# Value matmuls of 512 queries instead of 2 x 256, with new rules of the build-time scheduler, in a four-layer attention stack

## The chip, the cores and the metric

The kernel runs on one core of one Trainium2 chip. The metric is the device time of one execution in microseconds (us), the median of several runs. Besides these runs there is one profiled execution with a trace of every instruction of the engines: PE (matmuls; PEld are its weight loads), DVE (VectorE), ACT (ScalarE), POOL (GpSimd) and SP (which issues nearly all DMAs here).

## The reference

A sequence of 2048 tokens of width 512 goes through four layers A, B, A, B, each added to its input after a layer norm. Layer A is ordinary attention with 32 heads of width 16; layer B is a linear attention with a learned feature map ("Hedgehog").

```python
q, k, v = ...(x @ wqkv)                       # 32 heads, Dh = 16, S = 2048
# A:
scores = einsum("bhqd,bhkd->bhqk", q, k) * Dh ** -0.5
o = einsum("bhqk,bhkd->bhqd", softmax(scores), v);   out = o @ wo
# B:
phi_q = concat(softmax(q @ w_phi), softmax(-q @ w_phi));  phi_k likewise
kv = einsum("bhsf,bhsd->bhfd", phi_k, v);  z = sum_s phi_k
o = (phi_q @ kv) / (phi_q @ z + 1e-6);               out = o @ wo
x = x + A(ln(x)); x = x + B(ln(x)); x = x + A(ln(x)); x = x + B(ln(x))
```

## The kernel before, in words

What the change touches is `LayerA.attention`, which runs once for each of the two A layers. The work of one A layer is cut into 32 groups G; a group is a set of four heads (`g`, 8 of them) and a block of 512 queries (`j`, 4 of them). Inside a group a loop goes over 16 blocks of 128 keys (`kt`), and each key block has two halves of two heads. One half is one **tile**:

- `scores` (L1151): eight small f16 matmuls write the scores of 2 heads x 128 keys x 512 queries to one of two PSUM tiles `s`. I call these eight matmuls a score S. Two tiles `s` exist, so a score can only start when the exponential two tiles earlier has read its tile.
- one exponential on ACT (L1158) turns `s` into `p` (128 x 1024, f32) in SBUF. There are six buffers `p`.
- `pvs` (L1202) multiplies `p` by the values and adds to the group's accumulator: one call takes both halves of one key block, but only 256 of the 512 queries (`part` 0 or 1), in eight f32 matmuls. I call the work of both parts, a whole key block, a V; before, it is written as two halves. A buffer `p` is free when the V that reads it is done.

A layer has 32 x 16 x 2 = 1024 tiles. About one tile in 45 gets its exponential on DVE and POOL instead (`power_task`, buffer `px`); the rest are ACT's.

The accumulator of a group lies in one of two double banks of PSUM, called `double` and `pm` in the profile. The same two banks carry all **side products**: chains of up to twelve units of eight matmuls (`mm_cols`, L685) that compute q, k and v of the next heads or, late in a layer, the output projection; and the transposes of the next layer's input. `take` gives out a bank, `freed` gives it back when DVE has copied the result out of it. After a group's last V, DVE does that with two transposes (L850) in `norm_task`.

The order of all PE, DVE, ACT and POOL instructions is written out at build time (`tc.manual_schedule`): the loop in `attention` keeps a model clock for PE and ACT (`UNIT` is a score or a side unit, `PVHALF` half a V, `EXP` an exponential, `THERE` the time from a score's start to its exponential, `BACK` from an exponential's start to its tile `s` being free) and a second model, `Plan`, for DVE and POOL. At each step it emits a score if a tile is free, else a V, a side unit or a power score, if that fits before the next score is due. What the engines then do follows from the order and the semaphores alone; each engine runs its instructions strictly in order.

The output projection of a layer's first three quarters of the heads reads the normed outputs back from DRAM: `load_ob(j)` issues the DMA of `ob` (and, for j = 0, of the weights `woA`), and `part(j)` emits the side units that use it, 8 us of the model clock later.

In the first layer two more streams run beside the attention: `prep_b` (folds a feature map into weights of layer B, on PE and DVE, through the tiles `xt`) and `prep_rest` (splits the output weights of A, `prep_ao`, then the weights of B).

```python
            f = slice(256 * part, 256 * part + 256)
            ...
                    nc.tensor.matmul(acc[h][32 * hh:32 * hh + 32, f], self.oct[o]["v"][r, x:x + 32],
                                     pt[r, hh % 2, f], start=(kt == 0 and part == 0), stop=(kt == NT - 1), skip_group_check=True)
```

## Time and profile before

| | us |
|---|---|
| median of 3 runs | 2597.81 (2591.81 to 2602.13) |
| the profiled execution: time / span | 2605.12 / 2603.3 |
| mean granted PE clock, of full speed | 0.974 |
| busy in the span: PE / ACT / DVE / POOL | 2377.6 / 2135.1 / 1559.6 / 635.7 |
| ACT in the exponentials of L1158, 2003 of them: busy / idle before | 1852.3 / 111.3 |
| first layer A, first to last exponential | about 71 to 1057 |
| second layer A, first to last exponential | about 1377 to 2352 |

The two layers A take some 1960 of the 2603 us. A busy share is an average over stages: PE is shown busy in 91% of the span, but the matmuls' ends are modelled, and inside the layers A it is the chain of exponentials on ACT that has to be followed. An idle time in a row stands with what ended it ("<-PE s L1151": ACT waited for a score; "<-issue": the engine waited for nothing that the profile shows).

### The profile page before, as it was taken

How to read it: one execution, taken by the hardware profiler on the slowest of the kernel's cores; microseconds unless marked ns; L12 is line 12 of the kernel's file. 1: busy time of each engine (PE TensorE's matmuls, PEld its weight loads, DVE VectorE, ACT ScalarE, POOL GpSimd, SP SyncE). 2: the span in 40 equal slices, each digit the busy share in tenths (PEclk: the TensorE clock that was granted, in tenths of full speed). 3: DMA queues.
4: the chain of work that ended last, by engine and by line, in shares of the span. 5: the costliest groups of instructions: out<-in, count | busy, mean ns of one | idle time of the engine just before them, and what ended most of it. 6: DMA issues, size and time to landing. Idle time of an engine off the chain costs nothing.

```text
span 2603.3 us, 136308 instructions
## 1 busy us (share of the span) xinstructions
PE 2377.6 (91%) x63082; PEld 1380.2 (53%) x63082; DVE 1559.6 (60%) x2745; ACT 2135.1 (82%) x2381; POOL 635.7 (24%) x735
## 2 busy tenths in 40 slices
PE   6799999999988899899788999999899889998998
PEld 4466566555644555445345655565565556554543
DVE  8456556635664346889964564564455432557897
ACT  5799899999998899444437999999999889994453
POOL 3122222221120000356431222212121110004553
PEclk9899999999999999999888999999999999999999
DMA  5300421131044422100133003203300351210003
GB/s 195 59 18 8 92 54 38 29 50 35 5 103 112 157 96 68 50 17 17 66 100 53 18 8 61 33 5 48 66 5 12 75 143 53 69 52 25 9 17 107
DMA packets 114637, 144.96 MB, mean 56 GB/s; under 512 B 64152, under 2 KB 69896, under 8 KB 111624
## 3 DMA queue, kind: packets, MB, share of 16 engines
q1 hardware_dynamic: 112872, 133.38, 20.9%
q8 instruction: 495, 8.11, 1.3%
q0 software_dynamic: 1184, 2.77, 0.3%
q14 instruction: 86, 0.70, 0.1%
HBM read 62.16 MB, written 41.94 MB: 40 GB/s over the span
## 4 chain that ended last, share of the span: by engine, by line
ACT 46%; PE 24%; DVE 12%; issue 12%; SPq 3%; POOL 2%; DMA 1%; ACTq 0%; POOLq 0%; DVEq 0%
ACT p L1158 44%; PE s L1151 5%; PE pm L1202 4%; PE double L1202 3%; PE double L685 2%; PE pbv L1496 1%; DVE su L1566 1%; PE pk L1496 1%; PE po L668 1%; PE pm L685 1%; PE pq L1496 1%; SPq L863 1%; POOL f L1575 1%; DVE f L1558 1%; DVE st L474 1%
## 5 line engine op out<-in xcount | busy, mean ns | idle before, releaser
L1158 ACT ACTIVATE p<-s 128x1024 f32<-128x1024 f32 x2003 | 1852.3, 1106 | 111.3 <-PE s L1151 108.4
L1151 PE MATMUL s<-kq 49*32 49x512 f16 x15192 | 860.0, 386 | 63.3 <-ACT p L1158 17.4
L1202 PE MATMUL pm<-p,v 64*32 64x256 f32 x16592 | 693.1, 378 | 20.2 <-issue 19.9
L1151 PEld LDWEIGHTS <-kq 49*32 49x32 f16 x15872 | 392.7, 90 | 545.5 <-issue 407.5
L1202 PE MATMUL double<-p,v 64*32 64x256 f32 x15456 | 638.8, 380 | 3.7 <-issue 3.7
L1202 PEld LDWEIGHTS pm<-p,v 64*32 64x32 f32 x16592 | 349.0, 106 | 92.0 <-issue 34.7
L1202 PEld LDWEIGHTS double<-p,v 64*32 64x32 f32 x15456 | 320.8, 107 | 67.7 <-issue 14.1
L853 POOL TENSOR_TENSOR yt<-yt,yt 128x512 f32<-128x512 f32 x64 | 82.1, 1283 | 861.7 <-DVE yt L850 775.1
L1496 PEld LDWEIGHTS <-xnTa 128*128 128x128 f16 x1152 | 111.4, 99 | 157.3 <-DVE f L1559 29.8
L1235 DVE SCALAR_TENSOR_TENSOR xt<-double,c_oA,xt 128x512 f32<-128x512 f32 x78 | 58.1, 746 | 163.7 <-PE double L685 162.6
L1575 POOL TENSOR_TENSOR f<-f,su 128x1024 f32<-128x1024 f32 x62 | 119.8, 1933 | 132.4 <-DVE su L1569 106.1
L850 DVE STREAM_TRANSPOSE yt<-pm 128x512 f32<-128x512 f32 x66 | 43.7, 696 | 159.2 <-PE pm L1202 159.0
L850 DVE STREAM_TRANSPOSE yt<-double 128x512 f32<-128x512 f32 x62 | 41.2, 696 | 159.8 <-PE double L1202 159.8
L968 POOL TENSOR_TENSOR sq<-stg 128x512 bf16<-128x512 f16 x48 | 58.2, 1213 | 315.9 <-DVE stg L878 183.3
L1181 POOL TENSOR_TENSOR pz<-pw 128x512 f32<-128x512 f32 x90 | 103.5, 1151 | 128.3 <-DVE pw L1172 87.5
L685 PE MATMUL double<-woA,ob 64*32 64x512 f16 x2088 | 123.4, 378 | 1.7 <-issue 1.6
L1560 ACT ACTIVATE f<-f,c_pB 128x1024 f32<-128x1024 f32 x64 | 72.7, 1148 | 55.7 <-DVE f L1559 55.7
L1496 PE MATMUL pbv<-wbv,xnTa 128*128 128x512 f16 x384 | 95.4, 402 | 25.1 <-DVE f L1559 25.1
L685 PEld LDWEIGHTS <-wA 64*32 64x32 f16 x4608 | 86.4, 92 | 39.9 <-issue 2.7
L1183 DVE SCALAR_TENSOR_TENSOR px<-pz,px 128x512 f32<-128x512 f32 x90 | 82.2, 913 | 36.0 <-POOL pz L1181 28.6
L1581 ACT ACTIVATE fk<-f 128x1024 f16<-128x1024 f32 x30 | 31.7, 1057 | 72.2 <-POOL f L1575 72.2
L1496 PE MATMUL pq<-wbqk,xnTa 128*128 128x512 f16 x384 | 88.4, 379 | 0.0
(320 smaller groups left out, 3229.0 us busy)
## 6 DMA issues: line engine op xcount, KB each, us to landing
kq<-stg SPq DMA_DIRECT2D x168, 128.0 KB
xd<-xt SPq DMA_DIRECT2D x40, 512.0 KB
xt<-xd SPq DMA_DIRECT2D x40, 512.0 KB
v<-vyt SPq DMA_DIRECT2D x384, 16.0 KB
oD<-osp SPq DMA_DIRECT2D x24, 256.0 KB
ob<-oD SPq DMA_DIRECT2D x8, 768.0 KB
xt<-in_A_x_dram SPq DMA_DIRECT2D x8, 512.0 KB
wbqk<-dBqk SPq DMA_DIRECT2D x2, 2048.0 KB
```

The costliest lines, as they stand in the source:

```text
L685: nc.tensor.matmul(ps[h][c, :], w[r, c], x[r], start=(n == 0), stop=(n == of - 1), skip_group_check=True)
L850: nc.vector.transpose(ys[u].rearrange("p a b -> p (a b)"), ps[u])
L853: nc.gpsimd.tensor_tensor(ys[0], ys[0], ys[1], ALU.add)
L968: nc.gpsimd.tensor_tensor(sq, hi, hi, ALU.mult)
L1151: nc.tensor.matmul(banks2[u][32 * c:32 * c + 32, :], self.side(g, half, 64 * u, 0, kt * P + 32 * c, 32), self.side(g, half, 64 * u, 1, j * ...
L1158: nc.scalar.activation(pt, s, AF.Exp, scale=EXPS)
L1181: nc.gpsimd.tensor_tensor(z, w, w, ALU.mult)
L1183: nc.vector.scalar_tensor_tensor(y, z, PB, y, op0=ALU.add, op1=ALU.mult)
L1202: nc.tensor.matmul(acc[h][32 * hh:32 * hh + 32, f], self.oct[o]["v"][r, x:x + 32], pt[r, hh % 2, f], start=(kt == 0 and part == 0), stop=( ...
L1496: nc.tensor.matmul(dst, xnT[:, a, c, t * P:(t + 1) * P], w(b, c), start=(i == 0 and c == 0), stop=(i == 2 and c == NC4 - 1))
L1560: nc.scalar.activation(f, f, AF.Exp, scale=con["pB"])
L1575: nc.gpsimd.tensor_tensor(f3, f3, self.part_sums(f3, slice(0, 64), factor), ALU.mult)
```

## The change

One V is written as eight matmuls of 512 queries instead of sixteen of 256. With it, five things of the scheduler and its streams change:

- the model's numbers (`STEP` 0.865 for a whole V in place of twice `PVHALF` 0.434, `THERE`, `BACK`, `LATE`, and the new `SIDE` and `ALIGN`);
- a new side chain may take a bank right up to the end of a group (before, not at the group's last key block); no power tile in group 0;
- a side unit must end before the next `s` is free, not before the next score is due;
- `ob` for j = 0 is fetched from step 300 on, when the first output is stored (before: step 348), and its users come at least 22 us of the model clock after the fetch (14 for the others; before 8);
- `prep_ao` loads and splits the output weights in two halves, through the three `xt` tiles instead of two large ones, and runs after `prep_b` instead of before; the weights of B are loaded from step 356 on.

```diff
-PVHALF = 0.434
+STEP = 0.865
 EXP = 0.904
-THERE = 0.541
-BACK = 1.135
+THERE = 0.53
+BACK = 1.1
-AHEADS = 0
-LATE = 0.08
+LATE = 0.15
+SIDE = 0.0
+ALIGN = 0.05
...
     def prep_ao():
-        wo = load_w(a_wo, "awo")
+        ws = []
+        for i in range(2):
+            ws.append(xp.tile([P, 2, 512], F32, tag="xt", name=f"awo{i}"))
+            nc.sync.dma_start(ws[i], a_wo.rearrange("(c p) n -> p c n", p=P)[:, 2 * i:2 * i + 2])
...
+                    hl = xp.tile([P, 2, 2, 512], F16, tag="xt", name=f"ahlo{i}")
...
+            nc.sync.dma_start(dAo[:, :, 2 * i:2 * i + 2], hl)
...
     def prep_rest():
-        yield "until", lambda: a1.ready == 3
+        yield "until", lambda: bool(folded)
         yield from prep_ao()
-        yield "until", lambda: bool(folded)
+        yield "until", lambda: a1.now >= 356
...
-        def pvs(self, G, kt, part, acc):
+        def pvs(self, G, kt, acc):
...
-                    nc.tensor.matmul(acc[h][32 * hh:32 * hh + 32, f], self.oct[o]["v"][r, x:x + 32],
-                                     pt[r, hh % 2, f], start=(kt == 0 and part == 0), ...)
+                    nc.tensor.matmul(acc[h][32 * hh:32 * hh + 32, :], self.oct[o]["v"][r, x:x + 32],
+                                     pt[r, hh % 2, :], start=(kt == 0), ...)
...
         def part(self, j):
-                yield "gap", 8.0
+            yield "until", lambda: self.plan.now >= self.fetched[j] + (22.0 if j == 0 else 14.0)
...
-            events.append((348, lambda: "oA" in con, lambda: 0 in self.obs or self.load_ob(0)))
+            events.append((300, lambda: "oA" in con and self.ready == 3 and self.stored >= 0, lambda: 0 in self.obs or self.load_ob(0)))
...
-                    first = need is not None and need[1][0] == "pe" and (ready <= AHEADS or len(need[1]) > 2 and ready <= 3)
+                    first = need is not None and need[1][0] == "pe" and len(need[1]) > 2 and ready <= 1
...
-                                    soon = pvq and pvq[0][1] == NT - 1 or pvq and pvq[0][0] not in acc
+                                    soon = pvq and (NT - pvq[0][1] <= ALIGN * what[0] or pvq[0][0] not in acc)
...
-                                elif pe + what[0] <= max(due, free):
+                                elif pe + what[0] <= (free + SIDE if len(what) == 1 else max(due, free)):
...
-                            if (G in acc or min(self.pfree) <= pe) and pe + PVHALF <= max(due, free) + (LATE if ready > 1 else 0.0):
+                            if (G in acc or min(self.pfree) <= pe) and pe + STEP <= max(due, free) + LATE:
...
-                            if tried < G and G < POWERS and ...
+                            if tried < G and 0 < G < POWERS and ...
```

The new order, at three places. Rows that only repeat are left out ("...": the same weight load and matmul go on). First PE in the middle of a group of the first layer (`s` a score's tile, `kq` its operands, `double` here the group's accumulator, `wA`, `xnT` and `pm` a side product). Before:

```order
L1151 MATMUL s<-kq_1_990 32x512
L1202 MATMUL double<-p,v_162 32x256 x8
L685 LDWEIGHTS wA
L685 MATMUL pm_4788<-xnT_2_156,wA 32x512
...
L1151 LDWEIGHTS kq_0_989
L1151 MATMUL s<-kq_0_989 32x512
...
L1202 MATMUL double<-p,v_162 32x256 x8
```

After:

```order
L1165 MATMUL s<-kq_0_989 32x512
L1215 MATMUL double<-p,v_162 32x512 x8
L1165 LDWEIGHTS kq_1_990
L1165 MATMUL s<-kq_1_990 32x512
...
L699 LDWEIGHTS wA
L699 MATMUL pm_4901<-xnT_3_157,wA 32x512
...
L1165 LDWEIGHTS kq_0_989
```

Behind each score stood half a V and one side unit; now a whole V stands behind every second score and two side units behind the others.

Then PE at the border of groups 16 and 17 of the first layer, from the last V of the one to the first V of the other. Before (`pm` is the accumulator of both groups, `double` carries the side chain):

```order
L1202 MATMUL pm_14584<-px,v_6775 32x256
L685 LDWEIGHTS wA
L685 MATMUL double<-xnT_0_154,wA 32x512
...
L1151 MATMUL s<-kq_1_13594 32x512
...
L685 MATMUL double<-xnT_0_154,wA 32x512
...
L1151 MATMUL s<-kq_0_13593 32x512
...
L1151 MATMUL s<-kq_1_13594 32x512
L1202 MATMUL pm_15471<-p,v_6775 32x256
```

After (`double` is the accumulator of both, `pm` carries the side chain):

```order
L1215 MATMUL double<-px,v_5751 32x512 x4
L1165 LDWEIGHTS kq_0_11666
L1165 MATMUL s<-kq_0_11666 32x512
...
L699 MATMUL pm_13033<-xnT_0_154,wA 32x512
L1165 LDWEIGHTS kq_1_11667
L1165 MATMUL s<-kq_1_11667 32x512
L699 LDWEIGHTS wA
L699 MATMUL pm_13032<-xnT_0_154,wA 32x512
...
L1215 MATMUL double<-p,v_5751 32x512 x8
```

Before, three scores stand between the two V, the last two of them right ahead of the new group's first V. Now two scores do, and two side units stand between the second one and that V.

Last SP's queue where the output weights and the first outputs are fetched (`kq`: the next heads' operands, `bf`: weights of B, `oD`: outputs in DRAM). Before:

```order
L154 DMA awo<-in_A_wo_dram 128x4x512
...
L1138 DMA kq_1_20027<-sh 1x4x512 x4
L362 DMA dAo<-ahlo 128x4096
L435 DMA bf_20120<-dF_104 128x2048
L435 DMA bf_20121<-dF_105 128x2048
L689 DMA woA<-dAo 128x4096
L1209 DMA ob_20126<-oD 128x3072
```

After:

```order
L385 DMA dAo<-ahlo_9969 256x1x1024
...
L703 DMA woA<-dAo 128x4096
L800 DMA wAv<-dAv 128x1024
L957 DMA oD<-osp 128x1024
L1223 DMA ob_16271<-oD 128x3072
L449 DMA bf_16726<-dF_104 128x2048
L449 DMA bf_16727<-dF_105 128x2048
```

The weights are now stored two sets of operands (24 DMAs of `kq`) before `woA` is fetched, and `woA` and the first `ob` are ahead of the two loads `bf` that stood ahead of them.

More of the change, by code (lines that the diff above doesn't have):

```diff
@@ L323, in peaks @@
         for w in ws:
-            for d in range(NC4):
+            for d in range(w.shape[1]):
                 yield "V", 0.63, 3
@@ L835, in cols @@
         def cols(self, n, of, w, x):
-            yield "M",
+            yield "M", of
             idx, ps = self.take()
@@ L1201, in pvs @@
                     r = slice(64 * h, 64 * h + 64)
-                    nc.tensor.matmul(acc[h][32 * hh:32 * hh + 32, f], self.oct[o]["v"][r, x:x + 32],
-                                     pt[r, hh % 2, f], start=(kt == 0 and part == 0), stop=(kt == NT - 1), skip_group_check=True)
+                    nc.tensor.matmul(acc[h][32 * hh:32 * hh + 32, :], self.oct[o]["v"][r, x:x + 32],
+                                     pt[r, hh % 2, :], start=(kt == 0), stop=(kt == NT - 1), skip_group_check=True)
         def load_ob(self, j):
@@ L1208, in load_ob @@
             self.obs[j] = big([P, 3, 2, 512], F16, f"ob{j}")
+            self.fetched[j] = self.plan.now
             nc.sync.dma_start(self.obs[j], oD[j])
@@ L1437, in attention @@
                             G, kt, h = tiles[0]
-                            if tried < G and G < POWERS and pvdone >= G and kt <= 9 and min(self.pfree) <= pe and G in acc and pe + UNIT <= max(due, free):
+                            if tried < G and 0 < G < POWERS and pvdone >= G and kt <= 9 and min(self.pfree) <= pe and G in acc and pe + UNIT <= max(due, free):
                                 tried = G
```

48 lines of the change are left out of this document (27 added, 21 removed).

## The prediction, made before the change was run

> **What bounds the kernel.** I read the stage table first (busy us of each engine in four stretches of the span, in the order PE, PEld, DVE, ACT, POOL, then clock, DMA share, GB/s), then the costliest groups.
>
> ```profile
> 60.00:1100.00 1040.00, 962.62 (x29923) 577.19 (x29922) 581.82 (x1041) 941.95 (x1023) 188.16 (x195) 0.98 0.26 62
> 1370.00:2400.00 1030.00, 959.34 (x29879) 566.03 (x29878) 530.87 (x931) 945.81 (x1027) 189.10 (x185) 0.98 0.21 45
> L1158 ACT ACTIVATE p<-s 128x1024 f32<-128x1024 f32 x2003 | 1852.3, 1106 | 111.3 <-PE s L1151 108.4
> 2199.63 100.56 ACT L1158 ACTIVATE p<-s 128x1024 f32<-128x1024 f32 x109
> ```
>
> The change lives in the two layers A. There ACT is the bound: the last row, from the timeline of the second one, is 109 exponentials without a gap across three group borders, one every 0.92 us ((100.56 - 1.09) / 108). 2003 of them take some 1850 us whatever PE does. What the change can move is the 108.4 us in which ACT waited for a score. Where they lie, by the waits of four windows (70:130, 765:800, 1376:1430, 1990:2040; us, times, longest):
>
> ```profile
> ACT p L1158 <- PE s L1151: 13.5, 8, 9.6
> ACT p L1158 <- PE s L1151: 10.7, 2, 10.0
> ACT p L1158 <- PE s L1151: 11.4, 7, 7.2
> ACT p L1158 <- PE s L1151: 9.9, 6, 3.7
> ```
>
> The first and third are the starts of the layers, which the change leaves. The second and fourth hold the fetch of `ob`. The other 62.9 us (108.4 less these) are short waits. In PE's timeline they stand behind pauses that end with "issue", where PE waited for nothing that is recorded. 37 pauses of 0.35 us or more in the two layers add up to 44.5 us; the first, the longest and the last:
>
> ```profile
> 95.09 0.42 PE L1202 MATMUL double<-p,v 64*32 64x256 f32 x5 [0.44 <-issue]
> 892.27 0.42 PE L1202 MATMUL pm<-p,v 64*32 64x256 f32 x4 [2.60 <-issue]
> 2148.43 0.39 PE L1151 MATMUL s<-kq 49*32 49x512 f16 x2 [1.53 <-issue]
> 893.44 23.02 ACT L1158 ACTIVATE p<-s 128x1024 f32<-128x1024 f32 x25 [2.90 <-PE s L1151]
> ```
>
> The last row is ACT's wait behind the longest: 2.90 us for a pause of 2.60. What are they? Three stretches cut from one pause's end to the next, and the instruction queue of the page:
>
> ```profile
> 1628.90:1633.50 4.60, 3.81 (x128) 2.62 (x128) 4.39 (x6) 3.77 (x4) 2.75 (x2) 1.00 0.93 110
> 1633.50:1638.60 5.10, 3.81 (x128) 2.60 (x128) 2.64 (x4) 3.77 (x4) 0.00 (x0) 1.00 0.75 85
> 2107.65:2113.90 6.25, 3.72 (x126) 2.62 (x125) 0.00 (x0) 3.39 (x4) 0.00 (x0) 1.00 0.96 400
> q8 instruction: 495, 8.11, 1.3%
> q8 instruction: 11, 0.18, 2.0%
> ```
>
> 128 matmuls and 128 weight loads, 256 instructions, lie between two pauses (a few records are missing in the third). The queue moved 8.11 MB in 495 packets, 16.4 KB each, which is 256 instructions of 64 bytes. I read it so: PE's program arrives in pages of 256 instructions, the next is fetched while one runs (3.8 us), and where the data DMAs are busy (share 0.75 to 0.96) a fetch takes longer, 4.6 to 6.25 us, and PE stands. The last row is a quiet window (1700:1740): 11 pages in 40 us, and no pause.
>
> **The change part by part.** *Fewer instructions.* A V takes 64 PE instructions before: the trace has its f32 matmuls in two passes, each with its weight load (16 rows a half, as x16 shows below), and 32 after. The 32048 rows of L1202 and the 720 with `px` become half. Per two exponentials PE's stream falls from 128 (two scores 32, V 64, two side units 32) to 96, so a page lasts 5.3 exponentials, 4.9 us, in place of 3.7. A fetch may then take 1.2 us longer. Of the 37 pauses 15 exceed 1.2 us, and the excess sums to 9.1 of 44.5 us. ACT's loss to pauses I put at 55 of the 62.9 us (the rest stands at transposes and at waits of PE for DVE). Saved: 55 x (1 - 9.1/44.5) = **-44**. Bounds: -14 if only the number of pages falls (a quarter of 55), -50 if everything goes but the last few.
>
> *The steady order.* A V of 512 queries between two scores is the new rule; before, both halves stood together only here and there, as here:
>
> ```profile
> 767.64 0.38 PE L1202 MATMUL pm<-px,v 64*32 64x256 f32 x4
> 767.93 0.41 PE L1151 MATMUL s<-kq 49*32 49x512 f16 x8
> 768.12 1.31 DVE L850 STREAM_TRANSPOSE yt<-pm 128x512 f32<-128x512 f32 x2 [4.34 <-PE pm L1202]
> 768.14 1.06 PE L1202 MATMUL double<-p,v 64*32 64x256 f32 x32
> 769.01 0.41 PE L1151 MATMUL s<-kq 49*32 49x512 f16 x8
> 769.76 0.41 PE L1151 MATMUL s<-kq 49*32 49x512 f16 x8 [0.34 <-ACT p L1158]
> ```
>
> Score to score 1.08 us across the V, then 0.75 with a wait for ACT: 1.83, two beats of ACT. Two more numbers: from a score's start to its exponential, and from an exponential's start to the next score in its tile.
>
> ```profile
> 862.85 0.41 PE L1151 MATMUL s<-kq 49*32 49x512 f16 x7 [1.14 <-issue]
> 863.38 2.85 ACT L1158 ACTIVATE p<-s 128x1024 f32<-128x1024 f32 x3 [1.19 <-PE s L1151]
> 70.60 3.77 ACT L1158 ACTIVATE p<-s 128x1024 f32<-128x1024 f32 x4 [0.43 <-PE s L1151]
> 71.67 0.63 PE L1151 MATMUL s<-kq 49*32 49x512 f16 x8 [0.61 <-ACT p L1158]
> ```
>
> 0.54 (0.53 by the row, which lacks one matmul) and 1.07. A tile `s` is used every second beat, 1.83, so a score has 1.83 - 0.54 - 1.07 = 0.22 us of room, and two scores may lie 0.915 + 0.22 = 1.13 apart; the V asks 1.08. The two side units ask 0.21 + 0.44 = 0.65 of the other 0.75. It fits, by 0.05 us. I charge **+4** (bounds 0, as the rows show, and +20, were every second V late by 0.04).
>
> *The borders of groups.* Before, a border costs nothing (109 exponentials without a gap). After, I counted the order: 44 of the 62 borders have old and new accumulator in the same bank, and in 31 of them the first V has only one or two scores ahead of it and side units right before it. That V waits until DVE has read the old sums. By the rows above: last matmul of the old V at 767.64, PE free of it about 767.85, both transposes over at 769.43, so 1.6 us, with the release 1.65. Common form (score, two units, score, two units, V; clock from the old V's end): the second score must wait for its tile until 0.75, PE is at the V at 1.40, the V runs 1.65 to 2.51, the next score's exponential starts at 3.05, and was due at 2.42 (0.59 for the first, two beats later): 0.6 lost. With four to six units behind the second score PE gets there at 1.84 to 2.28: 0.8 to 1.25. With one score only: 1.5 to 1.85. By the counts, 13 x 0.6 + 13 x 1.0 + 5 x 1.6 + 1 = 30. DVE is not always free at once; it does its queue in order, and its subtraction of the operands, which stands right ahead of several of these transposes, is slow:
>
> ```profile
> L883 DVE TENSOR_TENSOR stg<-tq,stg 128x512 f16<-128x512 f32 x48 | 56.1, 1170 | 1.1
> ```
>
> I take a fifth more: **+36**. Bounds 20 (half the side units placed where PE idles anyway) and 55.
>
> *The outputs' fetch.*
>
> ```profile
> 775.41 0.42 SPq L1209 DMA_DIRECT2D ob<-oD  x1
> 784.97 0.63 PE L685 MATMUL pm<-woA,ob 64*32 64x512 f16 x8 [9.78 <-DMA ob<-oD]
> 2033.13 0.41 PE L685 MATMUL pm<-woA,ob 64*32 64x512 f16 x8 [3.58 <-DMA ob<-oD]
> ```
>
> The DMA needed 9.5 us, and the side unit stood at the head of PE with all scores behind it. Its users now come at least 22 us of the model clock after it, and `ob` is ahead of the loads `bf` on SP. Gone: 10.7 and 3.6, **-14**; bound -4 if queue and load stretch the fetch beyond 22 us.
>
> *The rest at nothing:* `prep_ao` in halves is the same DVE work, with two DMAs more on SP, far ahead of their reader; it hides under ACT's chain as before, and if SP held it up, `ob` would be late again. 44 power tiles in place of 45 cost ACT **+1**.
>
> Sum: -44 + 4 + 36 - 14 + 1 = -17 on the profiled execution's 2605.1, so 2588. That execution lies 7.3 above the median of the runs, 2597.8; for a timed run I forecast **2581**.
>
> **The rivals.** (1) *DVE late at the borders: slower.* If DVE comes to the transposes one subtraction of 1.17 us late at every one of the 31 borders, +36 becomes +72 and the time 2617. It turns from gain to loss at 1.7 us a border against my 1.2. For it: that row. Against: in the row at 768.12 DVE had been idle 4.34 us when the V ended, and rank 0 puts these transposes first.
> (2) *The pauses do not shrink.* If they come from something that is not paced by the page, say a fixed wait of the sequencer whenever DMA is busy, the -44 is missing: 2632, or 2625 for a timed run. For it: no row names the releaser. Against: the count of 256, and none in the quiet window. The Trainium skill, page "Runtime: NRT & Kernel Launch", section "Instruction fetch mechanics", speaks for this rival: it has blocks of 256 instructions, but calls the cost of crossing one mostly hidden, and gives PE room for 2048 instructions, so a run-out every 256 could not be; by that rule the sum is this rival's. Here 0.6 to 2.6 us stand at single crossings, so the trace agrees with the block and not with the hiding.
> (3) *Half the pauses go*, because a page's fetch starts late in the page before: -22 instead of -44, 2603, no change.
> (4) *Borders overlap with PE's spare time and cost the lower bound*, 20, and steady order 0: 2561.
>
> **How the numbers follow.** A measurement of this kernel can tell about 0.5%, 13 us, from no change. Chances: forecast 0.47 (own range 2570 to 2596), (1) 0.12, (2) 0.10, (3) 0.17, (4) 0.14. Under 2584.8 lie (4) and about three quarters of the forecast's own: faster 0.50. The rest of it and (3), same: 0.30. (1) and (2) are mostly beyond 2610.8: slower 0.20. The range 2560 to 2613 takes in (3), (4) and half of (1); (2) and the rest stay out.
>
> **What would show it.** PE's matmul rows 63082 to about 46700; the instruction queue 8.11 to about 6.0 MB; "issue" pauses fewer, at 256 instructions as before, under 1.5 us. New waits of the first V for DVE's transposes (`double` or `pm` from `yt`), 30 to 40 of them, each with an ACT wait of 0.6 to 1.9. No wait for `ob`. Between borders, no ACT gap in quiet stretches; gaps there would mean that the 0.05 us is not there, which at 0.05 for each of 1024 V is 51 us and the surest way to be wrong.

## The result, and the profile after

The changed kernel takes 2558.77 us (median of 4 runs, 2553.16 to 2562.03); the kernel before, run beside it, 2597.48. The ratio is 0.985, with a 95% interval of 0.9823 to 0.9876: 38.7 us faster, where 16.8 were forecast. Two later sets of runs gave 0.9823 (0.9801 to 0.9846) and 0.9832 (0.9816 to 0.9847). The profiled execution took 2557.37 us, its span 2555.6.

From the page of after: PE's busy time, the instruction queue (packets, MB) and the group of exponentials (busy, mean ns | ACT's idle time before them).

```profile
PE 2324.0 (91%) x46698; PEld 1090.4 (43%) x46698; DVE 1548.2 (61%) x2731; ACT 2134.2 (84%) x2382; POOL 633.0 (25%) x733
q8 instruction: 367, 6.01, 1.0%
L1172 ACT ACTIVATE p<-s 128x1024 f32<-128x1024 f32 x2004 | 1851.4, 1067 | 72.5 <-PE s L1165 70.4
```

A quarter of PE's instructions is gone (63082 to 46698 matmuls, 8.11 to 6.01 MB), with 54 us of its busy time, and the exponentials take what they took. What moved is ACT's idle time: 111.3 to 72.5, 38.8 us. From first to last exponential the first layer A lasts 968.5 us (before 986.3) and the second 953.0 (975.0): 17.8 and 22.0. The stretch between the two shrank as well, by 8.4 us (319.9 to 311.5), and the one behind the second did not change (251.5). That makes the 47.7 us between the two spans.

The pauses of PE that end with "issue", 0.35 us or more, in the layers A: before there were 37 of them, 44.5 us. After there are three, 3.85 us, and these are all:

```profile
830.87 0.40 PE L699 MATMUL pm<-woA,ob 64*32 64x512 f16 x5 [1.55 <-issue]
837.90 0.65 PE L1215 MATMUL double<-p,v 64*32 64x512 f32 x7 [1.14 <-issue]
1379.44 0.40 PE L1165 MATMUL s<-kq,kqe 49*32 49x512 f16 x5 [1.16 <-issue]
```

ACT's waits at the starts of the layers, in windows of about the length used before (70:130 and 1350:1405; us, times, longest):

```profile
ACT p L1172 <- PE s L1165: 1.5, 3, 0.8
ACT p L1172 <- PE s L1165: 4.4, 4, 2.0
```

They were 13.5 and 11.4, and the prediction had called them untouched. In PE's timeline of before, most of each is a wait of the power score (`pm<-kq,kqe`) for its operands `kqe`:

```profile
81.53 0.60 PE L1151 MATMUL pm<-kq,kqe 49*32 49x512 f16 x1 [7.46 <-DMA kqe<-sh]
1385.31 0.61 PE L1151 MATMUL pm<-kq,kqe 49*32 49x512 f16 x1 [5.11 <-DMA kqe<-sh]
```

No wait of PE for `ob` is left either. In their place stands one long new wait in the first layer A, seen on four engines (timelines of SP, DVE, PE and ACT; the bracket is the idle time before and what ended it):

```profile
118.67 25.18 SPq L877 DMA_DIRECT2D v<-vyt  x35
145.28 0.72 DVE L864 STREAM_TRANSPOSE yt<-double 128x512 f32<-128x512 f32 x1 [8.90 <-DMA v<-vyt]
146.98 0.63 PE L1165 MATMUL double<-kq,kqe 49*32 49x512 f16 x8 [7.66 <-DVE yt L864]
148.16 1.02 ACT L1172 ACTIVATE p<-s 128x1024 f32<-128x1024 f32 x1 [7.47 <-PE s L1165]
```

Read it from the top: SP issues 35 small transfers in a row, 0.7 us each. The sums `vyt` that they read lie in the same three buffers as `yt` and the copies `tq`, so DVE's next transpose into such a buffer stands; PE's power score needs the bank that DVE was to empty, so it stands with all scores behind it; so ACT stands. Two shorter new waits of ACT, 2.8 and 3.2 us, lie in the second layer A (at 1561 and 1740 us), where a side product waits until DVE has emptied its bank into `vyt`.

The borders of groups, in ACT's timeline:

```profile
1627.09 28.52 ACT L1172 ACTIVATE p<-s 128x1024 f32<-128x1024 f32 x31 [0.64 <-PE s L1165]
1685.69 28.55 ACT L1172 ACTIVATE p<-s 128x1024 f32<-128x1024 f32 x31 [0.91 <-PE s L1165]
234.86 1.09 PE L1215 MATMUL double<-p,v 64*32 64x512 f32 x16 [1.58 <-DVE yt L864]
```

Every 31 exponentials, which here is a group, ACT waits 0.6 to 0.9 us, where before 109 ran without a gap; the last row is one of the costlier borders, with the first V standing for DVE's transpose. Counted over the trace, ACT waits at 38 of the 62 borders, 36.1 us in all. Between borders there is no gap: (28.52 - 1.02) / 30 = 0.917 us from one exponential to the next.

The stretch between the layers: DVE's rows that close the last group of the first layer A, before (two rows, L928 and L936) and then after (L942 and L950).

```profile
1063.98 0.42 DVE L928 TENSOR_TENSOR yn<-yt,rec 128x256 f32<-128x256 f32 x1
1067.91 0.70 DVE L936 STREAM_TRANSPOSE yb<-yn 128x512 f32<-128x512 f32 x1
```

```profile
1044.25 0.42 DVE L942 TENSOR_TENSOR yn<-yt,rec 128x256 f32<-128x256 f32 x1
1045.19 0.70 DVE L950 STREAM_TRANSPOSE yb<-yn 128x512 f32<-128x512 f32 x1
```

The last exponential ended at 1056.86 and 1039.54, so the transpose on which the last quarter of the outputs hangs starts 11.1 us after it before, and 5.7 after. Before, DVE was still busy with the layer norm of the block ahead of it; after, those side products had been done earlier. 5.4 of the 8.4 us lie here. This belongs to the order: the transpose starts 11.1 to 11.2 us after the last exponential in all four profiles of kernels in the old order, and 5.6 to 5.8 us after it in all of the new order but the one in which transposes are doubled (7.8). Where the other 3 us lie was not found.

### The profile page after: what moved, and what is told of

It is laid out like the page before. It is cut to its first block, busy times and chain, and to the rows that moved or that the text cites. A ratio compares the mean times of both kernels' runs of the same rounds, so it can differ in the third digit from the quotient of the medians.

```text
span 2555.6 us, 103557 instructions
## 1 busy us (share of the span) xinstructions
PE 2324.0 (91%) x46698; PEld 1090.4 (43%) x46698; DVE 1548.2 (61%) x2731; ACT 2134.2 (84%) x2382; POOL 633.0 (25%) x733
## 3 DMA queue, kind: packets, MB, share of 16 engines
q8 instruction: 367, 6.01, 1.0%
## 4 chain that ended last, share of the span: by engine, by line
ACT 44%; PE 24%; DVE 13%; issue 11%; SPq 5%; POOL 2%; DMA 1%; ACTq 0%; DVEq 0%; POOLq 0%
ACT p L1172 42%; PE double L1215 5%; PE s L1165 4%; SPq L877 3%; PE pm L699 2%; PE pm L1215 2%; PE pbv L1509 2%; DVE su L1579 1%; PE pk L1509 1%; PE po L682 1%; PE pq L1509 1%; SPq L1152 1%; DVE f L1571 1%; PE double L699 1%; DVE f L1572 1%
## 5 line engine op out<-in xcount | busy, mean ns | idle before, releaser
L1172 ACT ACTIVATE p<-s 128x1024 f32<-128x1024 f32 x2004 | 1851.4, 1067 | 72.5 <-PE s L1165 70.4
L1165 PE MATMUL s<-kq 49*32 49x512 f16 x15168 | 788.6, 382 | 103.4 <-ACT p L1172 90.4
L1215 PE MATMUL double<-p,v 64*32 64x512 f32 x10768 | 737.7, 591 | 12.1 <-DVE yt L864 6.3
L1215 PE MATMUL pm<-p,v 64*32 64x512 f32 x5264 | 359.9, 592 | 0.0
L1215 PEld LDWEIGHTS double<-p,v 64*32 64x32 f32 x10768 | 207.9, 106 | 52.8 <-issue 13.7
L864 DVE STREAM_TRANSPOSE yt<-double 128x512 f32<-128x512 f32 x86 | 57.6, 698 | 222.5 <-PE double L1215 211.4
L1509 PEld LDWEIGHTS <-xnTa 128*128 128x128 f16 x1152 | 111.5, 99 | 156.9 <-DVE f L1572 28.1
L1249 DVE SCALAR_TENSOR_TENSOR xt<-pm,c_oA,xt 128x512 f32<-128x512 f32 x68 | 50.5, 743 | 107.9 <-PE pm L699 105.8
L1215 PEld LDWEIGHTS pm<-p,v 64*32 64x32 f32 x5264 | 101.8, 106 | 17.8 <-DVE yt L864 1.8
L699 PEld LDWEIGHTS <-wA 64*32 64x32 f16 x4608 | 75.8, 93 | 42.2 <-issue 4.1
L864 DVE STREAM_TRANSPOSE vyt<-pm 128x512 f32<-128x512 f32 x46 | 30.2, 692 | 96.6 <-PE pm L699 83.5
L1509 PE MATMUL pk<-wbqk,xnTa 128*128 128x512 f16 x384 | 88.1, 379 | 0.0
```

What stands on the lines that cost most here:

```text
L699: nc.tensor.matmul(ps[h][c, :], w[r, c], x[r], start=(n == 0), stop=(n == of - 1), skip_group_check=True)
L864: nc.vector.transpose(ys[u].rearrange("p a b -> p (a b)"), ps[u])
L1165: nc.tensor.matmul(banks2[u][32 * c:32 * c + 32, :], self.side(g, half, 64 * u, 0, kt * P + 32 * c, 32), self.side(g, half, 64 * u, 1, j * ...
L1172: nc.scalar.activation(pt, s, AF.Exp, scale=EXPS)
L1215: nc.tensor.matmul(acc[h][32 * hh:32 * hh + 32, :], self.oct[o]["v"][r, x:x + 32], pt[r, hh % 2, :], start=(kt == 0), stop=(kt == NT - 1), ...
L1509: nc.tensor.matmul(dst, xnT[:, a, c, t * P:(t + 1) * P], w(b, c), start=(i == 0 and c == 0), stop=(i == 2 and c == NC4 - 1))
```

## The experiments

Theory: PE's program comes in pages of 256 instructions, at a rate that the old stream of 128 instructions for two exponentials all but used up; fewer instructions remove the pauses. To this the side edits add or take away. The rival: it was the new order, or the place of the data transfers, that removed them.

### The same two kernels again

> The changed kernel as it is, beside the experiments, as their base. Its time should be 2559 us within 5. Open is the stretch between the two layers A (last exponential of the first to first exponential of the second): 319.9 us before, 311.5 after, though the change issues the same work there. Theory: the 8.4 us are a difference of single executions, since the profiled execution of before lay 7.3 us above the median of its runs and the one of after 1.4 below; this profile should then give another length than 311.5, between 310 and 320. Rival: the change itself shortens the stretch; then it is 311.5 within 1 us again.

> The changed kernel beside the two runs below, as their base: 2556 to 2562 us.

> The kernel before once more, for a second profile of it. Open is the stretch between the two layers A: 319.9 us in the first profile of before, 311.3 to 312.9 in four profiles of kernels after the change, but 317.4 and 315.0 in two others of them. Theory: it varies by execution; this profile gives another value than 319.9, between 311 and 318. Rival: it belongs to the old order; 319.9 within 1.5. The number of pauses of 0.35 us or more in the layers A should be near 37 and their sum near 44 again, within 8.

Measured: after 2560.09 and 2565.05 us (the second above what was expected), beside 2605.98 and 2607.24 of before. The stretch between the layers is 312.8 and 315.3 in these profiles of after and 319.0 in the second of before: it is shorter in the new order, and among three profiles of after it varies by some 4 us. The second profile of before shows 38 pauses, 49.1 us; the second and third of after show 6 and 2, 4.4 and 2.8 us.

### Each V as two halves again, in the new order

```diff
-                for h in range(2):
-                    nc.tensor.matmul(acc[h][32 * hh:32 * hh + 32, :], ..., pt[r, hh % 2, :], ...)
+                for f in (slice(0, 256), slice(256, 512)):
+                    for h in range(2):
+                        nc.tensor.matmul(acc[h][32 * hh:32 * hh + 32, f], ..., pt[r, hh % 2, f], ...)
```

> The changed kernel with each V issued as two halves of 256 queries, one right behind the other: the order of all units, the fetches and all other rules are those after; only the number of PE instructions is that of before again. Theory (pauses are paced by pages of 256 instructions): matmul rows near 63080, the instruction queue at 8.1 MB, some 30 to 45 pauses ending with issue of 0.35 us or more in the layers A with a sum near 40 us, and a time of 2595 to 2612 us, 36 to 53 above after. First rival (the pauses came from the old order of the units or from where the data DMAs stood): 3 to 6 pauses, 2559 within 8. Second rival (only the count of pages matters, each crossing with its own price): pauses grow by a third from 3 to 4 and the time by 2 us.

Measured: 2657.89 us, 97.8 above after and far above what was expected. Instruction queue and exponentials from the page, the first pause, and one group in ACT's timeline:

```profile
q8 instruction: 495, 8.11, 1.3%
L1172 ACT ACTIVATE p<-s 128x1024 f32<-128x1024 f32 x2004 | 1900.2, 1023 | 122.6 <-PE s L1165 117.0
92.56 0.40 PE L1216 MATMUL double<-p,v 64*32 64x256 f32 x1 [1.00 <-issue]
1692.01 29.30 ACT L1172 ACTIVATE p<-s 128x1024 f32<-128x1024 f32 x31 [0.73 <-PE s L1165]
```

The pauses are back, 27 of them, 26.7 us; the order is that of after, so the first rival is out, and the second (a third more of a small price) too. But they are less than half of the story. ACT's waits grew by 50.1 us and its busy time by 48.8: 31 exponentials take 29.30 us in place of 28.52, in a quiet stretch without a pause. Of the waits, those that stand within 3.3 us behind a stop of PE with "issue" (0.06 us or more) grew by 37 us, from 6.4 to 43.5. So the 98 us are some 37 that the theory asked for (36 to 53), some 13 of other waits, and about 49 that it had not. Late pages are not these 49: in the quiet stretch each page's packet of the instruction queue had landed 1.9 to 2.9 us before PE came to it, and a pause ends 1.2 to 1.8 us after such a landing.

### Half of the heads as halves

```diff
+                for f in (slice(0, 256), slice(256, 512)) if hh < 2 else (slice(0, 512),):
```

> The changed kernel with two of the four heads of each V issued as halves of 256 queries: 112 PE instructions for two exponentials, between the 96 after and the 128 of the run with all heads split, which took 98 us more. There a hole of 0.10 us stood in ACT's row after every 256 PE instructions (29.30 us for 31 exponentials in place of 28.52), and 27 pauses of 0.35 us or more came back. First theory (the hole is the price of each page, and the tight order passes it on whenever it comes): a page lasts 4.57 exponentials, 2004 of them hold 438 pages, 438 x 0.10 = 44 us, and some 15 for pauses: 2610 to 2625. Second theory (a page must last longer than what its fetch takes, some 3.8 us; here it lasts 4.2): hardly a hole, a few pauses, 2560 to 2580.

Measured: 2587.16 us, 27 above after.

```profile
q8 instruction: 431, 7.06, 1.1%
L1172 ACT ACTIVATE p<-s 128x1024 f32<-128x1024 f32 x2004 | 1854.7, 1046 | 100.6 <-PE s L1165 96.0
1651.93 28.52 ACT L1172 ACTIVATE p<-s 128x1024 f32<-128x1024 f32 x31 [0.71 <-PE s L1165]
```

The time lies between the two theories; the hole at every page is not there, since the pitch is after's 28.52 us. 12 pauses, 14.7 us, are back, and ACT's waits are 28.1 us above after. So in one order the pauses go with the number of instructions for two exponentials: 96, 112, 128 give 3, 12, 27 pauses and 3.9, 14.7, 26.7 us.

### Scores of two wide matmuls

```diff
-            for c in range(4):
-                for u in range(2):
-                    nc.tensor.matmul(banks2[u][32 * c:32 * c + 32, :], self.side(g, half, 64 * u, 0, kt * P + 32 * c, 32), ...)
+            for u in range(2):
+                nc.tensor.matmul(banks2[u], self.side(g, half, 64 * u, 0, kt * P, P), ...)
```

> The changed kernel with scores of two matmuls of 128 columns in place of eight of 32: 72 PE instructions for two exponentials in place of 96. Theory (at 96 the pages hardly bind any more: 3 to 5 pauses, 3 to 4 us): 2553 to 2560, at most 7 us gained, the instruction queue near 4.9 MB, no pause of 0.35 us or more. Rival (crossings still cost in the tight order): pitch under 28.5 us for 31 exponentials and 2535 to 2550. It also tells what a wide score costs PE, for the run with halves: if a score then takes PE more than 0.21 us, the pitch rises above 28.6.

> The run with every V in two halves (128 PE instructions for two exponentials, 98 us above the changed kernel), with one edit more: a score is two matmuls of 128 columns in place of eight of 32, so it takes 4 instructions for 16, and two exponentials 104. Theory (the 98 us are the pages: PE's program cannot be brought faster than 256 instructions in some 3.4 to 3.8 us, and a page would now last 4.5): the pitch between borders goes back to 28.5 us for 31 exponentials, few pauses of 0.35 us stay, the time is 2565 to 2590, near the 2587 of the run with 112. Rival (the halves themselves are slow on PE, whatever the number of instructions): 2640 or more. A third outcome, that wide matmuls are slower on PE than narrow ones, would show in the stretch from a score to the work behind it, 0.21 us now.

Measured: 2768.19 us with whole V, 2811.09 with halves. Both expectations missed, by the third outcome. PE's timeline, first with whole V, then with halves:

```profile
1609.97 0.39 PE L1164 MATMUL s<-kq 49*128 49x512 f16 x2
1610.29 1.09 PE L1214 MATMUL pm<-p,v 64*32 64x512 f32 x16
1611.32 0.39 PE L1164 MATMUL s<-kq 49*128 49x512 f16 x2
```

```profile
1614.01 1.14 PE L1215 MATMUL pm<-p,v 64*32 64x256 f32 x32
1615.07 0.39 PE L1164 MATMUL s<-kqe 49*128 49x512 f16 x2
```

A wide score holds PE for 0.32 us in place of 0.21, and the V before the next wide score for 1.03 in place of 0.86. The rows read as if narrow matmuls of one piece of work overlapped those of the next, and wide ones waited until all is through; no run tests that reading. Two things follow all the same. With 104 and with 72 instructions for two exponentials there is no pause of 0.35 us with "issue" in the layers A at all (these kernels are also slower, so a page lasts longer). And halves cost 42.9 us against whole V where there is no pause: 1.06 against 1.03 in these rows is 31 us for 1024 V. So halves have a price of their own where two of them stand together between two scores. Its size is near the 49 us that the first run with halves left over. That it is the same thing there is an inference, and not shown: in that run the stretch from V to score is 0.86 as after, and the lost 0.10 us stands in ACT's row at every fourth exponential.

### Edits beside the V: the rule on group 0, the transfers, the buffers

*No power tile in group 0, in the kernel before; and its opposite in the changed one.*

```diff
-                            if tried < G and G < POWERS and pvdone >= G ...
+                            if tried < G and 0 < G < POWERS and pvdone >= G ...
```

> The kernel before with one rule of the change alone: no power tile in group 0 (0 < G < POWERS). Theory: ACT's waits at the starts of the layers (13.5 and 11.4 us in the windows 70:130 and 1376:1430) fall to 2 to 4 each, the waits of PE for the DMA of kqe (7.5 and 5.1 us) vanish, and the time falls by 15 to 20 us against before. Rival: in the old order, with 128 PE instructions for two exponentials, the starts stay as long, since other work there waits for the same transfers: within 5 us of before. The stretch between the two layers A (319.9 us before, 311.5 and 312.8 after, 317.4 after with the power tile put back) tells besides whether this tile has to do with it: then it is near 312 here.

> The changed kernel with the power tile of group 0 let in again (G < POWERS in place of 0 < G < POWERS). Theory (this tile is what held PE for 7.5 and 5.1 us at the starts of the layers A before, because it reads kqe, which a DMA brings late): waits of PE for the DMA of kqe of 5 to 8 us at the two starts, ACT waits of 11 to 14 us in all at each start in place of 2 and 3, and a time 15 to 20 us above after, 2574 to 2579. Rival (the starts are short for another reason, as the order of the first side units, and the tile waits behind scores): 2559 within 4.

Measured: with the rule alone 2600.24 us, ratio to before 0.9977 (0.9958 to 0.9996), so 4.6 us only, where 15 to 20 were expected. With the tile let in again after the change 2578.85, 18.8 above the changed kernel beside it. ACT's waits of the kernel with the rule, its row of the wait at 152, and DVE's; then, of the changed kernel with the tile put back, two rows of PE and one of DVE:

```profile
ACT p L1158 <- PE s L1151: 13.5, 9, 8.1
152.40 1.02 ACT L1158 ACTIVATE p<-s 128x1024 f32<-128x1024 f32 x1 [8.08 <-PE s L1151]
149.55 0.75 DVE L873 TENSOR_SCALAR tq<-pm,c_qk 128x512 f32<-128x512 f32 x1 [9.08 <-DMA v<-vyt]
```

```profile
81.66 0.61 PE L1165 MATMUL pm<-kq,kqe 49*32 49x512 f16 x1 [6.31 <-DMA kqe<-sh]
1374.76 0.61 PE L1165 MATMUL pm<-kq,kqe 49*32 49x512 f16 x1 [4.16 <-DMA kqe<-sh]
603.96 0.75 DVE L887 TENSOR_SCALAR tq<-double,c_qk 128x512 f32<-128x512 f32 x1 [6.86 <-DMA v<-vyt]
```

The first row covers 70:160, where before has 14.5. In the windows of the starts the rule took ACT's waits from 13.5 and 11.4 to 3.8 and 7.9 us (70:130 and 1369:1424), and the work that it brought forward ran into the `v<-vyt` transfers: 8.1 of the gain came back as the same wait that after has.

Put back after the change, the tile brings its two waits for `kqe` back. But the 18.8 us are not these alone. The wait at 148 is then gone, so at the 101st exponential of the first layer A this kernel is only 1.2 us behind after. The rest comes later: DVE stands for `v<-vyt` at 604 us instead (the third row), the second layer is 7.5 us longer than in the first profile of after, and the stretch between the layers is 317.4 us. With the rule alone that stretch is 315.8 us, neither the 319.9 of before nor the 312 that would have laid the difference on the tile; what the tile has to do with it stays open.

Is the wait for `v<-vyt` the price of the early start? Three runs took it away.

*Half of those transfers from POOL, after; the same with the rule, before.*

```diff
-                    nc.sync.dma_start(dst[:, :, 33 * a + 1:33 * a + 33], yt[32 * a:32 * a + 32, m:16:4, :])
+                    (nc.sync if m < 2 else nc.gpsimd).dma_start(dst[:, :, ...], yt[...])
```

> The changed kernel with half of the transfers v<-vyt issued by POOL in place of SP. Theory: SP's row of 34 such issues in 24.5 us (from 119.31) holds a buffer yt, for which DVE's transpose waits 8.90 us, PE's score behind it 7.66 and ACT 7.47; with two queues this wait falls under 2 us, and the time by 6 to 10 us against the changed kernel, to some 2551. Rival: each issue costs POOL more than it costs SP, the sums of turned_sum and the squares on POOL come late, and the time is that of the changed kernel or up to 20 us more.

> The kernel before with two edits: no power tile in group 0, and half of the transfers v<-vyt issued by POOL. The first alone brought 5 us: ACT's waits at the starts fell by 15 us and one of 8.1 us came up at 152 us. Theory (that wait is the start's price, and comes from SP's row of transfers): it falls under 2 us, and the time is 11 to 16 us under before, ratio 0.994 to 0.996. Rival (what the start gains is lost further on in any case, since work that is earlier there meets the next limit): 3 to 7 us under before, with other waits in its place.

*A fourth buffer `yt`, after.*

```diff
-                ys.append(np_.tile([P, 16, 32], F32, tag="yb" if u else "yt", ..., bufs=2 if u else 3))
+                ys.append(np_.tile([P, 16, 32], F32, tag="yb" if u else "yt", ..., bufs=2 if u else 4))
...
```

> The changed kernel with four buffers yt in place of three (and three in place of four of the small buffers mx and mn of layer B, to make room). Theory (ACT's 7.5 and 1.1 us at 148 us are the wait of DVE's transpose for a buffer that transfers v<-vyt still read): that wait falls under 2 us, and the time is 6 to 10 us under the changed kernel beside it, 2549 to 2554. Rival (the queue of transfers is late by more than one buffer can hide, or layer B pays for mx and mn): within 4 us of the changed kernel.

Measured: 2554.81 us, ratio to before 0.9805 (0.9777 to 0.9833), for half the transfers from POOL after the change. The wait at 148 is gone, and at the 101st exponential this kernel is 9 us ahead of after; by the 501st other waits have taken some 6 of them back. The interval overlaps that of after (0.9801 to 0.9846), and while the first layer A is 3 to 4 us shorter than in the three profiles of after, the second is 3 to 6 longer: unclear as a gain. 2591.55 us, ratio 0.9946 (0.9929 to 0.9962), for the same with the rule before: 15.7 us under before, as the theory had it. 2545.71 us for the fourth buffer, 19.3 under the changed kernel beside it, twice what was expected. Waits of ACT in 70:160 with rule and POOL; then, with the fourth buffer, the exponentials and one row over the place:

```profile
ACT p L1158 <- PE s L1151: 5.9, 7, 2.9
```

```profile
L1172 ACT ACTIVATE p<-s 128x1024 f32<-128x1024 f32 x2004 | 1850.9, 1067 | 61.2 <-PE s L1165 58.9
128.97 31.34 ACT L1172 ACTIVATE p<-s 128x1024 f32<-128x1024 f32 x34
```

So rule and transfers together are worth 15.7 us, 11 more than the rule alone. Not all of the 11 is that wait: in the profiles ACT waits 12.8 us less in the layers A than with the rule alone, some 8 of them at the place; shorter pauses (41.9 us for 47.3) make up most of the rest, and in these the two profiles of before differ by over 4 us themselves.

With four buffers 34 exponentials run through the place without a gap. The first layer A is 12.5 us shorter than in the changed kernel beside it (955.6 for 968.1), the second 2.1. Of the 12.5, 9.8 are won by the 101st exponential, behind that place. Most of the rest is a second wait of the same kind, 450 us later. In the changed kernel beside it (rows of DVE and ACT) the copy `tq` stands for a buffer; with four (DVE's row below) it does not:

```profile
596.09 0.75 DVE L887 TENSOR_SCALAR tq<-pm,c_qk 128x512 f32<-128x512 f32 x1 [4.59 <-DMA v<-vyt]
598.93 1.02 ACT L1172 ACTIVATE p<-s 128x1024 f32<-128x1024 f32 x1 [3.94 <-PE s L1165]
```

```profile
584.87 0.75 DVE L887 TENSOR_SCALAR tq<-pm,c_qk 128x512 f32<-128x512 f32 x1
```

The other 7 us of the two spans lie outside the layers A, and nothing in the edit explains them; the kernel beside it had the longest stretches there of the three profiles of after (315.3 us between the layers A and 253.8 behind the second; 311.5 and 251.5 in the first profile, 310.8 and 250.5 with four buffers). This is the fastest version of all: ratio to before 0.9763 (0.9747 to 0.9778).

### The fetch of `ob`, the borders, and a shorter V

```diff
-            events.append((300, lambda: "oA" in con and self.ready == 3 and self.stored >= 0, ...))
+            events.append((348, lambda: "oA" in con, ...))
-            yield "until", lambda: self.plan.now >= self.fetched[j] + (22.0 if j == 0 else 14.0)
+                yield "gap", 8.0
```

> The changed kernel with the old rule for the fetch of ob (event 348, and a pause of 8 us of the model clock before the use, in place of event 300 and 22 or 14 us). Theory (the new rule is worth what the waits for ob were): waits of PE for ob of some 10 and 4 us, once in each layer A, and a time 10 to 14 us above after, 2569 to 2573. Rival (with fewer pauses the load is out of the way in any case): no wait for ob above 1 us, and 2559 within 4.

Measured: 2577.9 us, 17.8 above the changed kernel beside it, more than the 10 to 14 expected.

```profile
735.50 0.63 PE L1215 MATMUL pm<-p,v 64*32 64x512 f32 x4 [3.51 <-issue]
2014.41 1.06 PE L699 MATMUL double<-woA,ob 64*32 64x512 f16 x16 [4.37 <-DMA ob<-oD]
```

The waits return, one as a wait for `ob` and one as a page that comes late beside the transfers. The rest is the other order that the rule makes behind it; that part was not taken apart.

*Each transpose of finished sums done twice.*

```diff
                 nc.vector.transpose(ys[u].rearrange("p a b -> p (a b)"), ps[u])
+                if name == "yt":
+                    nc.vector.transpose(ys[u].rearrange("p a b -> p (a b)"), ps[u])
```

> The changed kernel with each of the two transposes of a finished group done twice by DVE, the second time with the same result; the planner's costs are not changed. It makes the release of the old sums 1.3 to 1.4 us later at each border. Theory (borders cost ACT some 33 us, since in 31 of 62 the first V waits for these transposes with little ahead of it): at those 31, 1.35 more each, and some 0.5 at the 13 others in the same bank: 45 us more than the changed kernel, 2595 to 2615. Rival (the small gaps at the borders come from the order of scores and side units, not from DVE): under 12 us more, 2560 to 2572.

Measured: 2638.8 us, 78.7 above the changed kernel (a run of another set); two borders in ACT's timeline:

```profile
1612.34 28.55 ACT L1174 ACTIVATE p<-s 128x1024 f32<-128x1024 f32 x31 [2.15 <-PE s L1167]
1643.01 28.52 ACT L1174 ACTIVATE p<-s 128x1024 f32<-128x1024 f32 x31 [2.12 <-PE s L1167]
```

1.5 us more at a border, at unchanged pitch between them. The borders do hang on DVE's transposes, and the rival is out. The time is above the range expected, since more borders than the 31 counted react once DVE is slower: in this trace ACT waits at 51 of the 62, 97.9 us in all, where after has 38 and 36.1.

*The last quarter of each V behind the next score.*

```diff
+                if hh == 3 and kt < NT - 1:
+                    self.rest4 = lambda pt=...: self.pv(G, kt, 3, pt, acc)   # issued behind the next score
+                    break
```

> The changed kernel with the last two of the eight matmuls of each V (not at the end of a group) issued behind the next score in place of ahead of it; the planner's numbers are not changed, and no instruction is added. Theory: in the steady order three exponentials are tied to a chain of PE and ACT: exponential to the score in its tile 1.13, score across the V to the next score 1.08, that score to its exponential 0.54, in all 2.75 us or 0.917 each, where ACT alone goes every 0.904 (before shows six in 5.42 us from 1725.27). With 0.22 us less across the V the chain is 2.53 and ACT is left alone: up to 0.013 x 2004 = 26 us less, so 2534 to 2550, with 28.1 us for 31 exponentials between borders. Rival: 0.917 is ACT's own pace in this program: 2560 within 6. Third: the borders or p's buffers, freed 0.9 us later, take it back: more waits of ACT at unchanged pitch, 2560 to 2575.

Measured: 2663.11 us, 103 above after; none of the three outcomes. PE's timeline from one score to the next:

```profile
1599.39 0.44 PE L1165 MATMUL s<-kq 49*32 49x512 f16 x8
1599.61 1.05 PE L1229 MATMUL double<-p,v 64*32 64x512 f32 x12
1600.44 0.44 PE L1165 MATMUL s<-kq 49*32 49x512 f16 x8
1600.66 1.02 PE L1229 MATMUL double<-p,v 64*32 64x512 f32 x4
1601.34 0.40 PE L1165 MATMUL s<-kq 49*32 49x512 f16 x6
```

Six of the eight matmuls take 0.83 us where eight took 0.86, and the two left behind hold PE for up to 0.68. The view ends within the last row. The eight write four blocks of 32 partitions side by side, and these times read as PE working on the blocks at once: here a V was not shortened by taking a block out of it. Whether the chain of 2.75 us for three exponentials holds ACT at 0.917 stays open.

## Why the prediction was right and wrong, point by point

**The pauses: the mechanism was right, the size too small.** -44 was forecast. ACT was taken to lose 55 us to pauses; the waits of ACT that stand behind a stop of PE with "issue" add up to 56.0 us before and 6.4 after: about -50. The prediction let 9.1 of the 44.5 us stay, because it took a fetch as late by a fixed time. Numbering PE's instructions in the traces by their start shows it closer: each of the pauses before (38; the prediction left out one of 0.36 us), of the 27 and 12 of the runs with halves and of the 3 after ends at the same place in a page of 256, 1.2 to 1.8 us after a 16.4 KB packet of the instruction queue has landed. So every pause is a page that came late, and rival (2) is out. How much was spare shows in the crossings without a pause: from the landing of the last packet to that place 1.7 us pass in the middle before, against 1.2 at the least behind a pause, so 0.5 us were left; after it is 3.6, so 2.4 are left, and of 335 crossings in the two layers three ran out of them. The Trainium skill, page "Runtime: NRT & Kernel Launch", section "Instruction fetch mechanics", calls the cost of crossing a block of 256 instructions mostly hidden; these runs differ, since 128 instructions for two exponentials in place of 96 bring 27 pauses in one order. A sentence further on there gives the instruction memory two lines of a page each, and with that the trace agrees: the packet of the next page starts some 1.0 us after a page is entered, in the middle before, and a late one stops PE at the very next crossing.

**The starts: the step that failed.** "The first and third are the starts of the layers, which the change leaves." It does not: the rule `0 < G` takes away the power tile of group 0, for which PE stood 7.5 and 5.1 us until a DMA had brought `kqe`, and the prediction had booked that rule as one power tile, +1 us. ACT's waits there fell from 24.9 to 5.9, -19. The prediction also missed the price, the `yt` wait at 148, about +9 with its echo. Net, after is 3.7 and 6.4 us ahead of before at the 101st exponential of the two layers, some 10 in all. In time the tile is worth 4.6 us in the kernel before, 15.7 together with the moved transfers, and 18.8 in the changed one; the last two hold other waits as well, as the experiments show.

**The steady order: right.** +4 was charged, 0 came: 0.917 from one exponential to the next, without gaps. Before it was 0.921 (the 109 exponentials).

**The borders: right, with a sign that did not show.** +36 forecast. Of ACT's 72.5 us of waits after, 36.1 lie at 38 of the 62 borders, at most 2.2 us each; doubling the transposes shows that they hang on DVE. The sign that was named, 30 to 40 waits of the first V for these transposes, shows in PE's own row only six times (6.3 us); the others show in ACT's row alone.

**The fetch of `ob`: right.** -14 forecast, and 10.7 and 3.6 are gone; undoing it costs 17.8 in time.

**What was not on the list:** the stretch between the layers A, put at nothing, 8.4 us shorter. 5.4 of them are the end of the first layer, where DVE's rows stand in another order; the other 3 stay open. The prediction had looked only between first and last exponential.

In ACT's time: -50 + 36 - 14 - 19 + 9 = -38, against 39.8 measured in the two layers. For the profiled executions the forecast was 17 less, and 47.7 came. Of the 31 between, these are 29: the starts with their price (10), the stretch between the layers (8), the pauses (6), the steady order (4) and the power tile (1). Between the medians the gap is 22, because the profiled execution of before lay 7.6 us above its median and that of after 1.4 below.

Of the rivals, (1) did not come: DVE was not a subtraction late at every border. (3) is out with the three pauses that are left. (4) named a time of 2561, near the one measured, and half of its cause is not there: the steady order did cost nothing, but the borders cost 36, not 20. So its nearness is luck.

## What to carry to other kernels

Count the instructions per unit of time of the engine that feeds the bound, not only its busy time. Here a PE page of 256 instructions lasted 3.7 us, hardly longer than its fetch, and data transfers showed as pauses without a releaser; a quarter fewer instructions took some 50 us of ACT's waits away. For each rule in a diff, also one that looks like housekeeping, find the row that it removes and ask what that row was holding up; and when work moves earlier, look which queue it joins: here 19 us came free, and 9 went to a wait for one of three buffers, which a fourth removed.

## What the hardware showed that was not expected

In and behind a long wait of PE the granted clock was half. Stretches of before and of after (busy us of PE, PEld, DVE, ACT, POOL; granted clock; DMA share; GB/s); the first holds the wait for `kqe` before (74.1 to 81.5), the second is the same stretch after, the third holds the `yt` wait after (139.3 to 147.0):

```profile
72.00:88.50 16.50, 8.04 (x145) 3.87 (x144) 5.10 (x8) 6.09 (x7) 2.31 (x3) 0.50 0.40 54
```

```profile
72.00:88.50 16.50, 15.54 (x353) 7.01 (x360) 2.06 (x5) 15.31 (x18) 1.93 (x5) 0.90 0.31 46
142.00:152.00 10.00, 5.02 (x72) 1.73 (x72) 6.69 (x11) 2.73 (x3) 3.49 (x3) 0.51 0.27 50
```

By the clock's record in the traces it was half from 71.3 to 88.3 us before, from the start of the layer to 6.8 us beyond the end of the wait, and from 141.5 to 151.8 after, 4.8 us beyond; without such a wait, in the second row, it was half only from 73.3 to 76.7, at the start of the layer, and full from there on. The Trainium skill, page "TensorE: Matmul & The Clock Gate", section "What's actually happening", has two states, half the clock after an idle window and the full one after a busy window; the rows agree (0.50 and 0.51 around the two waits). So a wait of PE can cost a little more than its length: behind the first, four more exponentials waited 0.2 to 0.3 us each, 1.05 us in all. And the form of a matmul matters beyond its work: a score of two matmuls of 128 columns held PE for 0.32 us and the V ahead of the next one for 1.03, where with eight of 32 columns it was 0.21 and 0.86.
